# Agent attention with a maxout layer: where the transfer buffers start in SBUF

## The chip, the cores and the metric

The kernel runs on one core of a Trainium2 chip. The metric is the device time of one execution in microseconds. Three runs of the kernel before took 255.32, 255.42 and 255.44 us; the median is 255.42 us.

## The reference

Four batches of 12,544 rows with 128 features, and 49 agent rows for each batch, all in fp32:

```
a2k     = softmax(agents @ k^T / sqrt(128))      # 49 x 12544 for each batch
agent_v = a2k @ v                                # 49 x 128
q2a     = softmax(q @ agents^T / sqrt(128))      # 12544 x 49
x       = q2a @ agent_v                          # 50176 x 128 over all batches
h       = max(x @ w1, x @ w2, x @ w3)            # 50176 x 768
out     = h @ w_out                              # 50176 x 128, fp32
```

## The kernel before, in words

Every row of x is a mean over 49 rows of agent_v with weights from q2a. The kernel therefore works on the 49 rows first: for most of the 768 hidden units one of the three branches is the largest for all 49 agents, and such a unit is linear in q2a. Only the units where the winner changes, at most 64 of them for a batch, are computed for every query; all that is linear is folded into one small matrix for each batch (G). Should there be more such units, or sums out of range, a branch at the end computes everything in the general way; in the runs shown it isn't taken.

**Keys.** For each batch, k and v come in 14 groups of 6 to 8 tiles of 128 rows. A load brings two or four groups at once: 14 or 28 rows for each of 128 partitions, which lie one after the other in HBM, so one partition's share is one run of 7,168 or 14,336 bytes. GpSimd (POOL) casts k and v to bf16 (KB, VB; for the first batch ScalarE casts v), TensorE (PE) turns k, VectorE (DVE) copies it out of PSUM (KT), PE makes the scores, ScalarE (ACT) their exponentials (EK), and PE adds them up with v.

**Queries.** 48 whole groups of 8 tiles, and a 49th group that is mixed: two tiles from each batch. One load brings three groups, 24 rows or 12,288 bytes for each partition; for the mixed group four runs of 1,024 bytes. POOL casts (QB), PE turns, ACT copies (QT), PE makes scores, ACT exponentials (EQ), PE the two branches that matter, ACT and DVE their maximum (AS, R), PE the output products, and DVE multiplies by one over the row's sum and writes fp32 to OS. One store sends three groups (12,288 bytes for each partition); the last ones are smaller.

**Order.** What each engine does in which order, and which buffer of a class each piece takes, is written out in a long string (ORDER) and not found at build time. All bulk transfers are issued by SP into one queue, 71 entries: 16 loads of k and 16 of v, 4 of weights, 17 of q, 18 stores. ACT issues one small load, of the agents, at the start. An entry waits on SP until its buffer is free, and the entries behind it wait too.

**Buffers.** `SLOTS` gives the number of buffers of each class, `SHAPE` their shape. The loads share five buffers LD of 14,336 bytes for each partition, the stores five buffers OS of 12,288 bytes. Line 217 allocates all classes in the order in which they stand in `SLOTS`; the constants (lines 218 to 282) lie ahead of them in SBUF, since their pool is opened first. Lines 316 (k, v), 376 (weights), 574 (q) and 577 (out) issue the transfers.

Of the kernel before, what the change touches and what calls it, by code (L numbers as in the profile page):

```python
# [16 lines left out]
P, H, C, A, B, NT, GT, KT, NF = 128, 64, 128, 49, 4, 98, 8, 7, 6  # L17
# [14 lines left out]

PE, ACT, DVE, POOL, SP = range(5)

SLOTS = {"M": 8, "LD": 5, "QB": 3, "KB": 3, "VB": 4, "KT": 3, "QT": 3, "EQ": 8, "EK": 4, "AS": 3, "R": 3, "OS": 5}
SHAPE = {"LD": ([P, max(TK * KT, LONG), C], FP32), "QB": ([P, GT, C], BF16), "KB": ([P, GT, C], BF16), "VB": ([P, GT, VC], BF16),
         "KT": ([P, GT * C], BF16), "QT": ([P, GT, P], BF16), "EQ": ([P, 512], BF16), "EK": ([P, GT * H], BF16),
         "AS": ([P, 512], BF16), "R": ([P, 512], BF16), "OS": ([P, LONG, C], FP32)}
# [2 lines left out]
class Plan:  # L41


    def __init__(self):
        self.ops, self.index, self.tiles, self.maker = [], {}, {}, {}
# [10 lines left out]
    def places(self, order, given):  # L56

        left = {}
        for o in self.ops:
            for t in o["use"]:  # L60
                left[t] = left.get(t, 0) + 1
        free = {c: list(range(n)) for c, n in SLOTS.items()}
        place = {}
# [12 lines left out]
def parts_of(s):  # L76

    if s < B * WHOLE:
        return [(s // WHOLE, s % WHOLE * GT, GT, 0, GT // 2)]
    return [(b, WHOLE * GT, 2, b, 1) for b in range(B)]  # L80
# [129 lines left out]
class Emit:  # L210
    def __init__(self, tc, pools, io):
        nc = tc.nc
        self.tc, self.nc, self.pools, self.io = tc, nc, pools, io
        self.t, self.place = {}, {}
        const = pools["const"]
        self.psum = pools["psum"].tile([P, 8, 512], FP32, name="psum")
        self.slots = {cls: [pools["sbuf"].tile(*SHAPE[cls], name=f"{cls}{i}") for i in range(n)] for cls, n in SLOTS.items() if cls != "M"}
        self.ident = const.tile([P, P], BF16, name="ident")
        make_identity(nc, self.ident)
        self.later = const.tile([P, P], BF16, name="later")  # L220
        make_lower_triangular(nc, self.later, diag=False)
        self.ones = const.tile([P, P], BF16, name="ones")
        nc.vector.memset(self.ones, 1.0)
        self.sums_of = const.tile([P, KEYS + NQ * GT], FP32, name="sums_of")
        nc.vector.memset(self.sums_of[:, :KEYS], 1.0)
        self.ag_st, self.ag_bf = self.slots["OS"][-1][:AP_, :A // 7, :], self.slots["QT"][-1][:AP_]
        nc.vector.memset(self.ag_bf, 0.0)
        nc.scalar.dma_start(self.ag_st, io["agents"].rearrange("b a c -> (b a) c").rearrange("(p j) c -> p j c", p=AP_))
        for e in self.slots["EK"]:
            nc.vector.memset(e, 0.0)  # L230
        for v in self.slots["VB"]:
            nc.vector.memset(v[:, :, C:], 1.0)
        self.agT = const.tile([P, B, H], BF16, name="agT")
        nc.vector.memset(self.agT, 0.0)
        self.sel = const.tile([P, 2], BF16, name="sel")
        nc.vector.memset(self.sel, 0.0)
        nc.vector.memset(self.sel[:A, 0:1], 1.0)
        nc.vector.memset(self.sel[H:H + A, 1:2], 1.0)
        self.ident_of_pairs = const.tile([P, P], FP32, name="ident_of_pairs")
        nc.vector.tensor_copy(out=self.ident_of_pairs, in_=self.ident)  # L240
        self.slot_of = const.tile([P, H], FP32, name="slot_of")
        self.avT = [const.tile([P, H], BF16, name=f"avT{b}") for b in range(B)]
        self.G = [const.tile([P, GC], BF16, name=f"G{b}") for b in range(B)]
        for t in self.avT + self.G:
            nc.vector.memset(t, 0.0)  # L245
        self.wo_bf = const.tile([P, NF, C], BF16, name="wo_bf")
        self.wall = const.tile([P, WC], BF16, name="wall")
        nc.vector.memset(self.wall[:, C1O:], 0.0)
        self.cand = const.tile([P, 3, NF, A], FP32, name="cand")
        flat = self.cand.rearrange("p i f a -> p (i f a)")  # L250
        self.w1_bf = flat[:, :DFF // 2].bitcast(BF16)
        self.w1T = flat[:, DFF // 2:DFF].bitcast(BF16).rearrange("p (f c) -> p f c", c=P)
        self.av, self.even_av = flat[:A, :C // 2].bitcast(BF16), flat[:A, C // 2:C // 2 + C + 1]
        self.uv, self.rp = (const.tile([P, NF, 2, H], BF16, name=n) for n in ("uv", "rp"))
        for t in (self.uv, self.rp):
            nc.vector.memset(t, 0.0)
        self.gap3 = const.tile([P, 3 * NF], FP32, name="gap3")
        self.gap = const.tile([P, NF], FP32, name="gap")
        self.open = const.tile([P, 2 * NF - 1], FP32, name="open")
        nc.vector.memset(self.open, 0.0)  # L260
        self.upto = const.tile([P, NF], BF16, name="upto")
        self.total = self.upto[:, NF - 1:]
        self.shut = const.tile([P, NF], FP32, name="shut")
        self.counts = const.tile([P, B], FP32, name="counts")
        self.good = const.tile([P, 2], FP32, name="good")
        self.good_bf = const.tile([P, 1], BF16, name="good_bf")
        self.most = const.tile([P, 1], INT32, name="most")
# [432 lines left out]
    def queries_in_general(self):  # L700
# [13 lines left out]
        for s in range(NQ):  # L714
            parts, half = parts_of(s), slice(s % TG * GT, (s % TG + 1) * GT)
            q, out = slots["LD"][3 + s % 2], slots["OS"][s // TG % SLOTS["OS"]]
            qb, qT, e, et = (slots[cls][s % 2] for cls in ("QB", "QT", "EQ", "AS"))
# [173 lines left out]
```

## Time and profile before

| what | value |
|---|---|
| median of three runs | 255.42 us |
| the profiled execution | 255.84 us |
| its span, first to last instruction | 254.0 us |
| DMA: bytes, packets | 104.85 MB, 11,067 |
| HBM read, written | 78.74 MB, 25.69 MB |
| share of 16 DMA engines taken by SP's queue | 97.9% |
| busy: PE, DVE, ACT, POOL | 78%, 66%, 59%, 66% |

The profile page lists the span in 40 slices with the busy share of the DMA engines (in tenths) and what they moved (GB/s). A row of the windows gives the busy time of each engine in a stretch, then the clock granted to TensorE, the DMA share and GB/s; the share can be a little over 1, as one packet begins just before the other ends. In a DMA answer for a window, "packets" counts every piece that a DMA engine moves, the small ones that report completion (under 512 B) too. "DMA ... to landing" is the time from issue to the last byte, queueing included.

### The profile page before, as it was taken

The page shows a single profiled execution, that of the slowest core. Times are in us where ns is not written, and L with a number is a line of the kernel's source. Part 1 is how long each engine was busy: PE and PEld are TensorE (multiplying, and loading weights), DVE is VectorE, ACT ScalarE, POOL GpSimd, SP SyncE. Part 2 cuts the span into 40 slices and gives each one's busy share as a digit, 9 for nine tenths or more (in the row PEclk, how much of TensorE's full clock was granted, in tenths as well). Part 3 has the DMA queues.
Part 4 walks back from the last instruction along what each step waited for, and adds up shares of the span by engine and source line. Part 5 has one row for each costly group of instructions (what it writes and reads, how often), then busy time and mean ns, then how long its engine had stood idle before and what let it go on. Part 6 is the DMA issues. An engine that isn't in the chain of part 4 may idle for free.

```text
span 254.0 us, 5192 instructions
## 1 busy us (share of the span) xinstructions
PE 199.2 (78%) x1899; PEld 144.1 (57%) x1899; DVE 167.7 (66%) x379; ACT 149.9 (59%) x252; POOL 168.3 (66%) x167
## 2 busy tenths in 40 slices
PE   0674687669899889898996898988787988999910
PEld 0462455547677567676774675856564555676600
DVE  8445512667678688767688964555738889888940
ACT  2346347248666776584765866556275868777620
POOL 2363643999899399998984988579484456548000
PEclk9999567799999999999999999799999999999995
DMA  6999999999999999999999999999999999999993
GB/s 240 432 420 425 419 424 428 424 423 423 427 418 427 436 417 425 423 425 427 412 431 426 426 429 423 427 428 423 418 431 421 433 413 422 430 426 424 424 415 147
DMA packets 11067, 104.85 MB, mean 413 GB/s; under 512 B 1150, under 2 KB 2174, under 8 KB 3866
## 3 DMA queue, kind: packets, MB, share of 16 engines
q1 hardware_dynamic: 10992, 104.34, 97.9%
q8 instruction: 17, 0.28, 0.4%
q14 instruction: 16, 0.13, 0.1%
q10 hardware_dynamic: 42, 0.10, 0.1%
HBM read 78.74 MB, written 25.69 MB: 411 GB/s over the span
## 4 chain that ended last, share of the span: by engine, by line
DMA 47%; POOL 17%; PE 15%; ACT 6%; DVE 5%; issue 5%; POOLq 0%; ACTq 0%; DVEq 0%
DMA LD<-in_k_dram 38%; PE psum L294 11%; DMA LD<-in_q_dram 9%; POOL KB L329 9%; POOL VB L329 6%; PE psum L340 4%; POOL QB L586 2%; ACT QT L592 2%; ACT EQ L605 2%; DVE OS L644 1%; DVE G L245 1%; ACT AS L625 1%; DVE KT L348 1%; DVE R L628 0%; ACT OS L647 0%
## 5 line engine op out<-in xcount | busy, mean ns | idle before, releaser
L586 POOL CAST QB<-LD 128x1024 bf16<-128x1024 f32 x49 | 60.6, 1266 | 36.8 <-DMA LD<-in_q_dram 23.5
L329 POOL CAST KB<-LD 128x1024 bf16<-128x1024 f32 (+1 forms) x56 | 62.7, 1160 | 26.7 <-DMA LD<-in_k_dram 26.7
L644 DVE TENSOR_TENSOR OS<-psum,sums_of 128x512 f32<-128x512 f32 x97 | 61.0, 677 | 5.5 <-PE psum L294 3.1
L592 ACT ACTIVATE QT<-psum 128x1024 bf16<-128x1024 bf16 x49 | 50.2, 1025 | 20.2 <-PE psum L340 18.1
L348 DVE COPY KT<-psum 128x1024 bf16<-128x1024 bf16 (+1 forms) x56 | 34.4, 621 | 32.0 <-PE psum L340 25.2
L340 PE MATMUL psum<-ident_of_pairs,KB 128*128 128x128 f32 x196 | 37.0, 314 | 6.5 <-POOL KB L329 5.1
L362 ACT ACTIVATE EK<-psum 128x392 bf16<-128x392 f32 (+1 forms) x56 | 25.8, 467 | 22.7 <-PE psum L294 9.8
L625 ACT ACTIVATE AS<-psum 128x512 bf16<-128x512 f32 x49 | 29.1, 599 | 16.8 <-PE psum L294 14.3
L628 DVE TENSOR_TENSOR R<-psum,AS 128x512 bf16<-128x512 f32 x49 | 32.6, 677 | 8.1 <-ACT AS L625 4.1
L294 PE MATMUL psum<-VB,EK 128*128 128x260 bf16 x196 | 33.8, 296 | 5.3 <-ACT VB L327 3.6
L329 POOL CAST VB<-LD 128x1024 bf16<-128x1024 f32 (+1 forms) x42 | 37.6, 941 | 0.0
L605 ACT ACTIVATE EQ<-psum 128x512 bf16<-128x512 f32 x49 | 29.3, 598 | 12.8 <-PE psum L294 12.4
L294 PEld LDWEIGHTS <-EQ 128*128 128x128 bf16 x392 | 27.5, 97 | 12.8 <-ACT EQ L605 7.7
L340 PE MATMUL psum<-ident_of_pairs,QB 128*128 128x128 f32 x196 | 31.7, 285 | 3.6 <-POOL QB L586 3.4
L340 PEld LDWEIGHTS psum<-ident_of_pairs,KB 128*128 128x128 f32 x196 | 24.6, 158 | 13.6 <-POOL KB L329 12.1
L294 PE MATMUL psum<-EQ,G 128*128 128x512 bf16 (+1 forms) x104 | 31.5, 365 | 0.9 <-ACT QT L592 0.7
L294 PE MATMUL psum<-G,R 128*128 128x256 bf16 x196 | 29.4, 273 | 1.2 <-DVE R L628 1.2
L294 PE MATMUL psum<-G,EQ 128*128 128x256 bf16 x196 | 29.6, 272 | 0.2 <-DVE OS L644 0.2
L340 PEld LDWEIGHTS psum<-ident_of_pairs,QB 128*128 128x128 f32 x196 | 21.7, 142 | 11.3 <-issue 5.2
L294 PEld LDWEIGHTS <-EK 128*128 128x128 bf16 x196 | 18.3, 103 | 14.7 <-issue 6.7
L294 PE MATMUL psum<-QT,agT 128*64 128x512 bf16 (+1 forms) x104 | 19.9, 385 | 6.7 <-ACT QT L592 6.4
L294 PE MATMUL psum<-agT,KT 128*128 128x49 bf16 x392 | 20.6, 191 | 4.0 <-DVE KT L348 3.7
(96 smaller groups left out, 166.9 us busy)
## 6 DMA issues: line engine op xcount, KB each, us to landing
LD<-in_q_dram SPq DMA_DIRECT2D x16, 1536.0 KB, 18.1
out_dram<-OS SPq DMA_DIRECT2D x15, 1536.0 KB, 21.0
LD<-in_k_dram SPq DMA_DIRECT2D x12, 1792.0 KB, 16.0
LD<-in_v_dram SPq DMA_DIRECT2D x12, 1792.0 KB, 16.3
LD<-in_k_dram SPq DMA_DIRECT2D x4, 896.0 KB, 16.1
LD<-in_v_dram SPq DMA_DIRECT2D x4, 896.0 KB, 14.1
LD<-in_moe_w_dram SPq DMA_DIRECT2D x3, 384.0 KB, 13.0
out_dram<-OS SPq DMA_DIRECT2D x2, 512.0 KB, 10.8
```

Source lines behind the costliest of these rows:

```text
L245: nc.vector.memset(t, 0.0)
L294: self.nc.tensor.matmul(out, w, x, start=start, stop=True, skip_group_check=True)
L329: self.nc.gpsimd.tensor_copy(out=out, in_=src)
L340: self.nc.tensor.transpose(t[:, i * P:(i + 1) * P], two[:, i * P:(i + 1) * P], self.ident_of_pairs)
L348: self.nc.vector.tensor_copy(out=self.t[f"kT{r}"][:, :n], in_=self.t[f"kT_ps{r}"].bitcast(BF16)[:, :n])
L362: self.nc.scalar.activation(e[:, :n, :A], s, AF.Exp, scale=SCALE)
L586: return lambda: self.nc.gpsimd.tensor_copy(out=two_by_two(self.t[f"qb.{s}"], GT), in_=self.half("q", s).rearrange("p (i x) c -> p i c x", ...
L592: return lambda: self.nc.scalar.activation(self.t[f"qT.{s}"].rearrange("p (x i) n -> p x (i n)", x=2), self.t[f"qT_ps.{s}"].bitcast(BF16). ...
L605: return lambda: self.nc.scalar.activation(self.t[f"e.{s}"], self.t[f"qs.{s}"], AF.Exp, scale=SCALE)
L625: return lambda: self.nc.scalar.activation(self.t[f"a.{s}"], self.t[f"u.{s}"], AF.Relu)
L628: return lambda: self.nc.vector.tensor_tensor(out=self.t[f"r.{s}"], in0=self.t[f"v.{s}"], in1=self.t[f"a.{s}"], op=ALU.max)
L644: self.nc.vector.tensor_tensor(out=out, in0=src, in1=rc.unsqueeze(2).to_broadcast([P, 4, C]), op=ALU.mult)
```

## The change

`SLOTS` names OS right behind LD, so the five store buffers follow the five load buffers in SBUF; all classes that stood between move up by 61,440 bytes. A constant tile of 192 bytes, which nothing reads or writes, moves everything that is allocated behind it by 192 bytes. Start addresses, in bytes of a partition, from the allocation of the two built programs:

| buffer | before | past a multiple of 256 / 512 | after | past a multiple of 256 / 512 |
|---|---|---|---|---|
| LD0 | 39,232 | 64 / 320 | 39,424 | 0 / 0 |
| LD4 | 96,576 | 64 / 320 | 96,768 | 0 / 0 |
| OS0 | 162,240 | 192 / 448 | 111,104 | 0 / 0 |
| OS4 | 211,392 | 192 / 448 | 160,256 | 0 / 0 |
| QB0 | 110,912 | 64 / 320 | 172,544 | 0 / 0 |
| R2 | 161,216 | 192 / 448 | 222,848 | 128 / 128 |
| agT | 18,880 | 192 / 448 | 19,072 | 128 / 128 |

LD1 to LD3 and OS1 to OS3 lie between at whole multiples of 512 from their neighbours. On every engine the instructions, their order and their waits are the same in both programs; only addresses differ, and lines behind the inserted one have a number that is higher by one.

```
-SLOTS = {"M": 8, "LD": 5, "QB": 3, "KB": 3, "VB": 4, "KT": 3, "QT": 3, "EQ": 8, "EK": 4, "AS": 3, "R": 3, "OS": 5}
+SLOTS = {"M": 8, "LD": 5, "OS": 5, "QB": 3, "KB": 3, "VB": 4, "KT": 3, "QT": 3, "EQ": 8, "EK": 4, "AS": 3, "R": 3}
...
         self.sums_of = const.tile([P, KEYS + NQ * GT], FP32, name="sums_of")
+        const.tile([P, 192], mybir.dt.uint8, name="pad")
         nc.vector.memset(self.sums_of[:, :KEYS], 1.0)
```

## The prediction

> **What bounds the kernel now.** I read the page first, for the DMA engines, because the change moves buffers that only transfers of q, k, v, the weights and the output fill and empty in bulk.
>
> ```profile
> DMA  6999999999999999999999999999999999999993
> GB/s 240 432 420 425 419 424 428 424 423 423 427 418 427 436 417 425 423 425 427 412 431 426 426 429 423 427 428 423 418 431 421 433 413 422 430 426 424 424 415 147
> DMA packets 11067, 104.85 MB, mean 413 GB/s; under 512 B 1150, under 2 KB 2174, under 8 KB 3866
> q1 hardware_dynamic: 10992, 104.34, 97.9%
> ```
>
> In 38 of 40 slices the 16 DMA engines are busy nine tenths or more, and one queue's packets (q1, SP's) alone take 97.9% of what 16 engines have over the span. Next come the windows (columns: PE, PEld, DVE, ACT, POOL busy with counts, granted clock, DMA share, GB/s), to see whether any stretch has another limit.
>
> ```profile
> core 0: us, PE busy (x) PEld busy (x) DVE busy (x) ACT busy (x) POOL busy (x), PEclk, DMA share, GB/s
> 30.00:40.00 10.00, 7.55 (x61) 5.25 (x59) 2.37 (x4) 5.20 (x9) 5.17 (x5) 0.67 1.01 426
> 50.00:60.00 10.00, 7.12 (x81) 5.29 (x80) 6.68 (x20) 6.17 (x14) 9.98 (x10) 1.00 0.99 419
> 180.00:200.00 20.00, 15.43 (x143) 10.86 (x141) 13.54 (x28) 10.98 (x18) 11.26 (x10) 1.00 1.01 428
> 220.00:230.00 10.00, 9.59 (x91) 6.55 (x90) 8.86 (x18) 8.21 (x13) 4.75 (x4) 1.00 1.01 424
> 240.00:245.00 5.00, 2.45 (x19) 1.48 (x16) 4.38 (x14) 1.74 (x5) 0.00 (x0) 1.00 1.03 417
> 245.00:250.00 5.00, 0.00 (x0) 0.00 (x0) 0.00 (x0) 0.00 (x0) 0.00 (x0) 0.74 0.87 357
> ```
>
> Where POOL is full (50 to 60 us) or PE nearly so (220 to 230 us), the DMA share is still about 1: the queue is never empty behind them. After 245 us no engine computes and the transfers still run. So the time is what the DMA engines need for 104 MB, and compute only has to issue early enough. The chain and SP's queue say the same of the end:
>
> ```profile
> 132.48 22.03 DMA LD<-in_k_dram
> 159.00 23.04 DMA LD<-in_q_dram
> ...
> 243.51 1.14 ACT OS L647 x4
> ```
>
> ```profile
> L574 SPq DMA_DIRECT2D LD<-in_q_dram x17: 327/328/3565, 35.0 to 198.1; - x17
> L577 SPq DMA_DIRECT2D out_dram<-OS x18: 332/398/3442, 68.8 to 244.7; - x18
> DMA packets 384, 2.47 MB, mean 247 GB/s; under 512 B 46, under 2 KB 56, under 8 KB 184
> out_dram<-OS SPq DMA_DIRECT2D x1, 512.0 KB, 8.4
> ```
>
> The first two rows say when SP issued its loads of q and its stores, first and last (us). The other two are of the window 244 to 254 us: 2.47 MB were still to move when the last store was issued at 244.7 us, 5.8 us at 424 GB/s, and that store landed 8.4 us after its issue. The chain leaves the DMA at 182 us (159.00 + 23.04) for a compute stretch, but this backlog lies behind it. A DMA that is up to about 4 us faster over the program ends about that much earlier; one that is slower ends later in full. Nothing else covers it.
>
> **The change part by part.** No instruction, wait, queue entry or byte is added or removed; only start addresses move. Compute tiles move by 192 bytes (the constants behind the pad) or by 61,632 (QB to R), and OS moves by -51,136. All three are multiples of 64 (3, 963 and 799 times), so no engine operand changes its place within 64 bytes. I price this part at nothing; if it cost, the rows above say that compute may finish some 4 us later before the backlog is gone. SP still issues the same 71 entries in the same order, and the pad is written by nobody.
>
> What can move is the cost of a run, the contiguous piece (one per partition, or several) that a DMA engine moves as one packet. The issues give the number of runs:
>
> ```profile
> LD<-in_q_dram SPq DMA_DIRECT2D x16, 1536.0 KB, 18.1
> out_dram<-OS SPq DMA_DIRECT2D x15, 1536.0 KB, 21.0
> LD<-in_k_dram SPq DMA_DIRECT2D x12, 1792.0 KB, 16.0
> LD<-in_v_dram SPq DMA_DIRECT2D x12, 1792.0 KB, 16.3
> LD<-in_k_dram SPq DMA_DIRECT2D x4, 896.0 KB, 16.1
> LD<-in_v_dram SPq DMA_DIRECT2D x4, 896.0 KB, 14.1
> LD<-in_moe_w_dram SPq DMA_DIRECT2D x3, 384.0 KB, 13.0
> out_dram<-OS SPq DMA_DIRECT2D x2, 512.0 KB, 10.8
> out_dram<-OS SPq DMA_DIRECT2D x1, 1024.0 KB, 9.3
> LD<-in_q_dram SPq DMA_DIRECT2D x1, 512.0 KB, 22.1
> LD<-in_moe_w_out_dram SPq DMA_DIRECT2D x1, 384.0 KB, 13.5
> ```
>
> Loads: 16 + 24 + 8 + 4 = 52 with 128 runs, and the 512 KB one of q with 4 x 128, so 7,168 or 448 for each engine. Stores: 15 + 1 + 1 with 128, and one of the two 512 KB stores (the mixed group) with 512, so 2,688 or 168 for each engine. Together 616.
>
> What a run costs beyond its bytes comes from three windows: loads alone (30 to 65 us), the mixed group's load, which has runs of 1,024 bytes (206 to 208 us), and stores alone (225 to 235 us; the last load of q, issued at 198.1 us, has landed by then, 26.8 us later by its row).
>
> ```profile
> DMA packets 1207, 14.89 MB, mean 426 GB/s; under 512 B 129, under 2 KB 129, under 8 KB 131
> q1 hardware_dynamic: 1202, 14.84, 100.3%
> DMA packets 309, 0.80 MB, mean 398 GB/s; under 512 B 16, under 2 KB 265, under 8 KB 265
> q1 hardware_dynamic: 309, 0.80, 100.8%
> DMA packets 390, 4.28 MB, mean 428 GB/s; under 512 B 42, under 2 KB 42, under 8 KB 42
> q1 hardware_dynamic: 389, 4.26, 100.6%
> DMA to landing us min/median/max: 26.8/26.8/26.8
> ```
>
> Stores: 10 us x 16 x 1.006 = 161.0 engine-us for 389 - 42 = 347 runs of 12,288 bytes, 463.9 ns each with its share of the small completion packets. The middle window: 2 x 16 x 1.008 = 32.26 engine-us for 265 - 16 = 249 runs of 1,024 bytes and 44 of 12,288; 32.26 - 44 x 0.4639 leaves 47.6 ns for a short run. The slope is (463.9 - 47.6) / 11,264 = 0.0370 ns a byte, and a run of no bytes would cost 47.6 - 37.9 = 9.7 ns. That is all that a start address can be charged with here: at most 616 x 9.7 ns = 6.0 us. The other end is nothing, or below it (the second rival).
>
> Which end is nearer? Before the change every load run starts 64 bytes past a multiple of 256, every store run 192 past. Loads alone: 35 x 16 x 1.003 = 561.7 engine-us for 1,073 runs of 13,830 bytes on average, 523.5 ns, of which the slope explains 511.2 and 12.3 ns are left (1,207 - 129 less the 5 packets of other queues are the 1,073 runs). Two quite different misplacements therefore have remainders that are close, 12.3 and 9.7 ns, and the order is the wrong one: a cost by misplaced bytes would make the stores 128 x 0.0370 = 4.7 ns dearer, and they are 2.6 ns cheaper. A cost common to both, or one of the loads alone, cannot be excluded from these rows, as no run here starts on a boundary. I take nothing, because the one comparison of two placements that the trace offers speaks against a charge, and keep 6.0 us for the range. A gain of 0.51 us (0.2%, the least this kernel's measurement tells from no change) needs 0.83 ns a run.
>
> By the Trainium skill, "DMA: Bandwidth & Descriptors", section "How a descriptor splits into AXI transactions", a read begins at the multiple of 256 bytes below its start, and the bytes ahead of the start are fetched for nothing and still take their beats. Taken for both directions, it is the second form of the first rival. The same page (section "Where 436 GB/s comes from") puts the ports' ceiling at 435 GB/s; beside the 426 measured, this leaves some 2%, an estimate of 5 us from that figure; the trace agrees in size with its bound of 6.0 us.
>
> Sum: 0 for compute, 0 for issue, 0 for the runs. The profiled execution took 255.84 us, its span 254.0, so 1.84 us lie around it; the median of the runs is 255.42, 0.42 below the profiled one, and the forecast stands at the median: **255.4 us**, with 255.0 to 255.8 as its own range.
>
> **The rivals.** First, a run that starts off a boundary is charged for the misplaced bytes, and the change takes that away. If only loads pay (their target is SBUF, and their remainder is the higher one), the price is the 64 misplaced bytes, 64 x 0.0370 = 2.4 ns: 448 runs make 1.1 us, so 254.3 us. For it speaks that loads are dearer by just 2.6 ns; against it, that loads also have another source, HBM, which can explain the same, and that the difference of two remainders from rounded shares is no sharp number. If both pay, stores at 192 x 0.0370 = 7.1 ns, 168 runs add 1.2 us: 255.4 - 1.1 - 1.2 = 253.1 us. Against this stands the stores' remainder of 9.7 ns, of which 2.6 would be left for the rest, where loads keep 9.9.
>
> Second, on the other side: after the change all ten buffers start at the same place within 512 bytes, where loads stood at 320 and stores at 448. If a write to one and a read of another meet more often in the same part of a partition's memory, transfers of both directions slow each other. The place is the mixed stretch, from the first store (68.8 us) to the last load's issue (198 us), 129 us. The price I take from the slowest loads-only row above, 419 GB/s, against some 425: 1.4% of 129 us, 1.8 us, so 257.2 us. It decides from 0.4% on (0.51 of 129 us), as no other work covers the queue. Against it: five load buffers share one phase today, and reads of POOL and writes of DMA at that phase show no loss at 426 GB/s.
>
> Third, that the change doesn't do what it says, would leave 255.4 as well; the built program's addresses are multiples of 512, so I give it no chance of its own.
>
> **How the numbers follow.** No effect that can be measured 0.46; loads alone gain 0.24 (254.3); loads and stores gain, or more up to the bound, 0.13 (253.1 and below); slower 0.17, by the second rival or something like it in a part of its size. So faster by over 0.2% (below 254.9) has 0.37, within 0.2% 0.46, slower 0.17. The range goes from 252.9, which holds the first rival in both forms, to 256.6, which holds the second rival up to two thirds of its price: **252.9 to 256.6 us**.
>
> **What would show it.** In the profile after, the rows of the same three kinds of windows: loads alone, short runs, stores alone. I expect remainders again near 12 and 10 ns, 426 GB/s, and 97.9% for q1. If the loads' remainder falls by some 2.4 ns and the stores' does not, the first form of the first rival holds; if both fall, the second. If only mixed windows lose GB/s, it is the second rival. The largest groups of compute should keep their means (677, 1160 and 1266 ns) to a per cent:
>
> ```profile
> L644 DVE TENSOR_TENSOR OS<-psum,sums_of 128x512 f32<-128x512 f32 x97 | 61.0, 677 | 5.5 <-PE psum L294 3.1
> L329 POOL CAST KB<-LD 128x1024 bf16<-128x1024 f32 (+1 forms) x56 | 62.7, 1160 | 26.7 <-DMA LD<-in_k_dram 26.7
> L586 POOL CAST QB<-LD 128x1024 bf16<-128x1024 f32 x49 | 60.6, 1266 | 36.8 <-DMA LD<-in_q_dram 23.5
> ```
>
> Wrong altogether would be a time that moves while all these remainders stay: then compute or issue limits a stretch in which I read the queue as full.

## The result, and the profile after

The changed kernel takes 254.29 us (median of 14 runs) against 255.6 for the kernel before in the same comparison; the ratio of the one to the other is 0.9934, 95% interval 0.9915 to 0.9953. So it is faster by 0.66%, 1.7 us (1.2 to 2.2). The ratio is of the means of the undisturbed runs (254.14 and 255.82 us); two slow runs of the changed kernel, of 259.67 and 263.2 us, count in its median alone, so the medians lie only 1.3 us apart. The time lies in the range and 1.1 us below the forecast of 255.4; the first form of the first rival, "loads alone gain", had 254.3.

The page of the changed kernel, its DMA lines:

```profile
DMA  6999999999999999999999999999999999999994
DMA packets 11067, 104.85 MB, mean 416 GB/s; under 512 B 1150, under 2 KB 2174, under 8 KB 3866
q1 hardware_dynamic: 10992, 104.34, 98.1%
```

The same packets and bytes, the engines as full as before, and a higher rate: each packet has become cheaper. The windows say where. First three stretches of the kernel before, then of the changed one (last two columns: DMA share, GB/s):

```profile
10.00:65.00 55.00, 40.55 (x382) 29.96 (x381) 26.42 (x53) 29.46 (x53) 36.32 (x34) 0.84 1.01 424
65.00:180.00 115.00, 102.22 (x1036) 76.09 (x1034) 82.32 (x177) 73.93 (x127) 96.24 (x93) 0.99 1.01 424
180.00:240.00 60.00, 51.90 (x459) 34.65 (x458) 47.73 (x105) 42.43 (x66) 32.22 (x31) 1.00 1.01 425
```

```profile
10.00:65.00 55.00, 40.20 (x386) 29.07 (x386) 26.06 (x54) 30.35 (x53) 36.93 (x35) 0.91 1.01 428
65.00:180.00 115.00, 101.14 (x1021) 75.06 (x1030) 82.74 (x178) 73.25 (x126) 95.41 (x92) 0.99 1.01 428
180.00:240.00 60.00, 52.44 (x452) 35.35 (x457) 46.67 (x103) 42.41 (x66) 32.27 (x31) 0.97 1.01 426
```

424 has become 428 GB/s as long as loads make up most of the queue, and 425 only 426 in the last stretch, where the loads run out and stores fill it. The DMA answers for windows give it by run. Of the changed kernel, loads alone (30 to 65 us), then stores alone (226 to 236 us):

```profile
DMA packets 1213, 15.02 MB, mean 429 GB/s; under 512 B 128, under 2 KB 128, under 8 KB 128
q1 hardware_dynamic: 1208, 14.96, 100.3%
DMA packets 384, 4.23 MB, mean 423 GB/s; under 512 B 40, under 2 KB 40, under 8 KB 40
q1 hardware_dynamic: 383, 4.21, 99.5%
```

Loads: 35 x 16 x 1.003 = 561.7 engine-us for 1,208 - 128 = 1,080 runs of 13,852 bytes, 520.1 ns a run, where 523.5 ns stood for 13,830 bytes. The 22 bytes more are worth 0.8 ns at the prediction's 0.0370 ns a byte, so a load run is 4.2 ns cheaper. Stores: 159.2 engine-us for 343 runs, 464.1 ns where 463.9 stood: unchanged. From 10 to 65 us, with more runs, the same for the kernel before and the changed one:

```profile
DMA packets 2322, 23.32 MB, mean 424 GB/s; under 512 B 256, under 2 KB 256, under 8 KB 768
q1 hardware_dynamic: 2316, 23.24, 100.5%
...
DMA packets 2336, 23.52 MB, mean 428 GB/s; under 512 B 256, under 2 KB 256, under 8 KB 768
q1 hardware_dynamic: 2330, 23.44, 100.4%
```

256 packets of each are completion reports. 884.4 engine-us for 2,060 runs are 429.3 ns, of which 12.3 remain when the bytes (11,282 at 0.03696 ns, 417.0 ns) are taken off; 883.5 for 2,074 runs are 426.0, and 8.3 remain. So 4.0 ns less for each load run; 448 runs for each DMA engine make 1.8 us, which is the measured gain within its interval. The remainders themselves hang on the slope, which joins short load runs to long store runs; what counts here is their difference between two kernels.

Compute didn't change and didn't gain. The largest groups of the changed kernel keep their means (1264, 1154 and 678 ns for 1266, 1160 and 677), and its last piece of work starts at 243.59 us, where the kernel before had it at 243.51 (below, in this order: the groups, the end of the chain, the landing of the stores):

```profile
L587 POOL CAST QB<-LD 128x1024 bf16<-128x1024 f32 x49 | 60.6, 1264 | 37.1 <-DMA LD<-in_q_dram 21.1
L330 POOL CAST KB<-LD 128x1024 bf16<-128x1024 f32 (+1 forms) x56 | 62.5, 1154 | 26.5 <-DMA LD<-in_k_dram 26.0
L645 DVE TENSOR_TENSOR OS<-psum,sums_of 128x512 f32<-128x512 f32 x97 | 61.0, 678 | 5.0 <-PE psum L295 3.1
...
243.59 1.14 ACT OS L648 x4
...
DMA to landing us min/median/max: 5.7/17.9/26.2
```

The last row is of the stores: the quickest to land, which is the last one, now needs 5.7 us instead of 8.4. So the gain came out of the backlog behind the last compute.

### The profile page after: what moved, and what is told of

The parts are those of the page before. It is cut to its first block, busy times and chain, and to the rows that moved or that the text cites. A ratio compares the mean times of both kernels' runs of the same rounds, so it can differ in the third digit from the quotient of the medians.

```text
span 252.0 us, 5173 instructions
## 1 busy us (share of the span) xinstructions
PE 198.4 (79%) x1880; PEld 142.9 (57%) x1899; DVE 166.8 (66%) x379; ACT 150.1 (60%) x252; POOL 167.9 (67%) x167
## 4 chain that ended last, share of the span: by engine, by line
DMA 48%; POOL 17%; PE 12%; ACT 5%; issue 4%; DVE 2%; POOLq 0%; ACTq 0%; DVEq 0%
DMA LD<-in_k_dram 31%; DMA LD<-in_q_dram 17%; PE psum L295 10%; POOL KB L330 9%; POOL VB L330 7%; PE psum L341 2%; ACT QT L593 2%; POOL QB L587 1%; ACT EQ L606 1%; DVE OS L645 1%; ACT cand L391 1%; DVE R L629 0%; ACT OS L648 0%; ACT AS L626 0%; DVE G L550 0%
## 5 line engine op out<-in xcount | busy, mean ns | idle before, releaser
L587 POOL CAST QB<-LD 128x1024 bf16<-128x1024 f32 x49 | 60.6, 1264 | 37.1 <-DMA LD<-in_q_dram 21.1
L330 POOL CAST KB<-LD 128x1024 bf16<-128x1024 f32 (+1 forms) x56 | 62.5, 1154 | 26.5 <-DMA LD<-in_k_dram 26.0
L593 ACT ACTIVATE QT<-psum 128x1024 bf16<-128x1024 bf16 x49 | 50.2, 1024 | 20.0 <-PE psum L341 19.2
L341 PE MATMUL psum<-ident_of_pairs,KB 128*128 128x128 f32 x196 | 35.6, 306 | 5.0 <-POOL KB L330 3.2
L363 ACT ACTIVATE EK<-psum 128x392 bf16<-128x392 f32 (+1 forms) x56 | 25.8, 467 | 20.9 <-PE psum L295 12.5
L295 PE MATMUL psum<-VB,EK 128*128 128x260 bf16 x196 | 33.1, 291 | 6.1 <-ACT VB L328 4.1
L295 PEld LDWEIGHTS <-EQ 128*128 128x128 bf16 x392 | 28.2, 98 | 13.0 <-ACT EQ L606 7.6
L295 PE MATMUL psum<-G,R 128*128 128x256 bf16 x196 | 30.7, 281 | 1.2 <-DVE R L629 1.2
L295 PE MATMUL psum<-G,EQ 128*128 128x256 bf16 x196 | 31.1, 282 | 0.0
L341 PEld LDWEIGHTS psum<-ident_of_pairs,KB 128*128 128x128 f32 x196 | 23.6, 153 | 12.3 <-POOL KB L330 9.8
L295 PE MATMUL psum<-EQ,G 128*128 128x512 bf16 (+1 forms) x85 | 25.8, 363 | 1.9 <-ACT QT L593 0.7
```

The source lines that it names most:

```text
L295: self.nc.tensor.matmul(out, w, x, start=start, stop=True, skip_group_check=True)
L330: self.nc.gpsimd.tensor_copy(out=out, in_=src)
L341: self.nc.tensor.transpose(t[:, i * P:(i + 1) * P], two[:, i * P:(i + 1) * P], self.ident_of_pairs)
L363: self.nc.scalar.activation(e[:, :n, :A], s, AF.Exp, scale=SCALE)
L587: return lambda: self.nc.gpsimd.tensor_copy(out=two_by_two(self.t[f"qb.{s}"], GT), in_=self.half("q", s).rearrange("p (i x) c -> p i c x", ...
L593: return lambda: self.nc.scalar.activation(self.t[f"qT.{s}"].rearrange("p (x i) n -> p x (i n)", x=2), self.t[f"qT_ps.{s}"].bitcast(BF16). ...
```

## The experiments

The three theories of the first four: **A**, only where a load's run starts in SBUF counts; **B**, loads and stores both pay for a start off a boundary; **C**, the store buffers' place next to the load buffers does it. In each case the remainder of a run is worked out from q1's row of 10 to 65 us as above (packets less 256; share x 880 engine-us; less 0.03696 ns a byte, the slope of the prediction unrounded). A rounded share is good to about 0.2 ns and the rounded MB to 0.1 ns.

**The pad alone** (`SLOTS` as in the kernel before; loads at multiples of 512, stores 128 past a multiple of 256):

```
+        const.tile([P, 192], mybir.dt.uint8, name="pad")
```

> The pad alone: load buffers at multiples of 512, store buffers stay last, now 128 past a multiple of 256. Theory A (only where a load's run starts in SBUF counts, some 4 ns for each of 448 load runs an engine): all of the gain, ratio to before about 0.993, q's queue moves 23.44 MB in 10 to 65 us as in the changed kernel (23.24 before). Theory B (loads and stores both pay for a start off a boundary): only part of it, the stores 128 past still pay; 0.995 or above. Theory C (the store buffers' place next to the load buffers brings it, not the boundary): ratio 1.000, 23.24 MB.

Measured: 253.89 us, ratio 0.9922 (0.9893 to 0.9951), the whole gain. Its row of 10 to 65 us:

```profile
q1 hardware_dynamic: 2334, 23.50, 100.5%
```

884.4 / 2,078 runs is 425.6 ns, remainder 7.6. That is A's figure; the move of the store buffers isn't needed.

**Stores alone on the boundary**, by 64 bytes ahead of them at their old place:

```
-SLOTS = {..., "R": 3, "OS": 5}
+SLOTS = {..., "R": 3, "PAD": 1, "OS": 5}
-         "AS": ([P, 512], BF16), "R": ([P, 512], BF16), "OS": ([P, LONG, C], FP32)}
+         "AS": ([P, 512], BF16), "R": ([P, 512], BF16), "PAD": ([P, 16], FP32), "OS": ([P, LONG, C], FP32)}
```

> Store buffers alone at multiples of 512, by 64 bytes of padding ahead of them at their old place; load buffers as before, 64 past a multiple of 256. Theory A: ratio 1.000, 23.24 MB in 10 to 65 us, a store run 464 ns in 225 to 235 us. Theory B: faster by up to 0.5% (168 store runs an engine at 7 ns are 1.2 us), a store run some 457 ns. Theory C: 1.000.

Measured: 255.36 us, ratio 0.9984 (0.9965 to 1.0003), no difference that this comparison tells. Rows of 10 to 65 us and of 226 to 236 us:

```profile
q1 hardware_dynamic: 2316, 23.24, 100.5%
...
DMA packets 393, 4.26 MB, mean 426 GB/s; under 512 B 47, under 2 KB 47, under 8 KB 47
q1 hardware_dynamic: 392, 4.24, 100.1%
```

The load row is to the digit that of the kernel before, and a store run costs 160.2 / 345 = 464.2 ns, as it did 192 bytes past a boundary (463.9). B falls: stores, which read SBUF, pay nothing.

**The order alone** (OS behind LD, no pad; all ten 64 past a multiple of 256):

```
-SLOTS = {"M": 8, "LD": 5, "QB": 3, ..., "R": 3, "OS": 5}
+SLOTS = {"M": 8, "LD": 5, "OS": 5, "QB": 3, ..., "R": 3}
```

> Store buffers behind the load buffers without the pad: all ten 64 past a multiple of 256, 320 past one of 512. Theory A: ratio 1.000, 23.24 MB in 10 to 65 us. Theory B: 1.000 or a little faster, as stores go from 192 to 64 past. Theory C: all of the gain, 0.993. The rival that equal phases of loads and stores slow the mixed stretch: slower than before, at a DMA rate below 424 GB/s in 65 to 180 us.

Measured: 255.89 us, ratio 0.9988 (0.9968 to 1.0008). Rows of 10 to 65 us and 65 to 180 us:

```profile
q1 hardware_dynamic: 2315, 23.23, 100.5%
...
DMA packets 4404, 48.79 MB, mean 424 GB/s; under 512 B 490, under 2 KB 490, under 8 KB 1037
```

Remainder 12.5 ns, as before: C falls. Here all ten buffers stand at one phase, with loads and stores mixed from 68.9 us on, and the rate is the 424 GB/s that the kernel before has there: the prediction's second rival falls as well, at this phase; in the changed kernel, with all ten on the boundary, that stretch rose to 428.

**Multiples of 256 alone** (the changed kernel with 448 bytes of padding, all ten 256 past a multiple of 512):

```
-        const.tile([P, 192], mybir.dt.uint8, name="pad")
+        const.tile([P, 448], mybir.dt.uint8, name="pad")
```

> As the changed kernel, with 448 bytes of padding in place of 192: all ten buffers at 256 past a multiple of 512, that is at multiples of 256 alone. If the boundary that counts is 256 or less: ratio 0.993, 23.44 MB in 10 to 65 us. If it is 512: ratio 1.000 or above, 23.24 MB or less.

Measured: 253.87 us, ratio 0.9919 (0.9893 to 0.9945).

```profile
q1 hardware_dynamic: 2334, 23.50, 100.5%
```

Remainder 7.6 ns. 512 isn't the boundary; 256 is enough.

**How the charge goes with the distance.** Three kernels differ from the changed one in the pad alone: 320 bytes (128 past a multiple of 256), 128 bytes (192 past) and 224 bytes (32 past); the first is shown.

```
-        const.tile([P, 192], mybir.dt.uint8, name="pad")
+        const.tile([P, 320], mybir.dt.uint8, name="pad")
```

> As the changed kernel with 320 bytes of padding: all ten buffers 128 past a multiple of 256. Theory A1 (a load run pays for the bytes between the boundary of 256 below it and its start): twice the charge of 64 bytes, 8 ns a run, 3.6 us over the changed kernel, ratio to before 1.007, 23.04 MB in 10 to 65 us. Theory A2 (a fixed charge for any start off a multiple of 256): as before, 1.000, 23.24 MB. Theory A3 (the boundary that counts is 128): as the changed kernel, 0.993, 23.5 MB.

> As the changed kernel with 128 bytes of padding: all ten buffers 192 past a multiple of 256. Theory A1: three times the charge, 12 ns a run, 5.4 us over the changed kernel, ratio to before 1.014, 22.85 MB in 10 to 65 us. Theory A2: as before, 1.000, 23.24 MB. Theory A3: 64 past a multiple of 128, as before, 1.000, 23.24 MB. The stores stand where they stood before, 192 past.

> As the changed kernel with 224 bytes of padding: all ten buffers 32 past a multiple of 512. Compute tiles behind the pad move by 32 within 64 bytes as well. Theory A1: half the charge, 2 ns a run, 0.9 us over the changed kernel, ratio to before 0.997, 23.35 MB in 10 to 65 us. Theory A2 and A3: the full fixed charge, 1.000, 23.24 MB; more than that if the boundary of 64 counts too, 1.003 or above.

Measured: 255.43 us, ratio 0.9987 (0.9963 to 1.0011) at 128 past; 256.41 us, 0.9997 (0.9977 to 1.0017) at 192 past; 256.63 us, 1.0026 (1.0002 to 1.0051) at 32 past. Rows of 10 to 65 us in the same order:

```profile
q1 hardware_dynamic: 2317, 23.26, 100.5%
...
q1 hardware_dynamic: 2314, 23.21, 100.4%
...
q1 hardware_dynamic: 2315, 23.23, 100.7%
```

| load runs start past a multiple of 256 by | kernel | ns a run | remainder, ns | one run of 14,336 bytes, ns | ratio to before |
|---|---|---|---|---|---|
| 0 | changed | 426.0 | 8.3 | 535.0 | 0.9934 |
| 0 | the pad alone | 425.6 | 7.6 | 535.0 | 0.9922 |
| 0 (256 past 512) | pad 448 | 425.6 | 7.6 | 535.0 | 0.9919 |
| 32 | pad 224 | 430.4 | 13.4 | 540.8 | 1.0026 |
| 64 | before | 429.3 | 12.3 | 539.7 | 1 |
| 64 | stores alone | 429.3 | 12.3 | 539.8 | 0.9984 |
| 64 | order alone | 429.5 | 12.5 | 539.7 | 0.9988 |
| 128 | pad 320 | 429.1 | 12.0 | 538.9 | 0.9987 |
| 192 | pad 128 | 429.3 | 12.5 | 539.7 | 0.9997 |

The last column but one is the mean of the longest load runs, from the trace's records of single packets (runs that took over 1.2 times the median are left out, 0.5% of these at most, and some 4% at most of the other lengths below). Two levels, and about a nanosecond within the upper one: A2. A charge by misplaced bytes (A1) would put 192 three times as high as 64, and the 128 boundary (A3) would bring the gain at 128. At 32 past, a run costs about 1 ns more than at 64 and the ratio lies just over 1, and at 128 past the longest runs are 0.8 ns cheaper; with one trace of each, and compute tiles 32 past a multiple of 64 in the first, what this last nanosecond is stays open.

An engine that reads the load buffers isn't needed for the charge: POOL's first cast starts at 6.0 us (6.2 in the changed kernel), and of the runs of 7,168 bytes that began before 5.9 us the median is 278 ns in the kernel before and 272 in the changed one.

**A charge for each run, or for the bytes?** A fixed 4 ns for runs of some 14 KB could also be 0.9% of the bytes. So each load of k, v and whole q was issued as two, with half of each partition's run, once off the boundary (from the kernel before) and once on it (from the changed kernel; the halves are multiples of 256 long). The edit for k and v, which q has in the same way but for its mixed group:

```
-            self.nc.sync.dma_start(self.t[f"{which}{b}.{g}"][:, :n * KT, :], src)
+            cut = n * KT // 2
+            self.nc.sync.dma_start(self.t[f"{which}{b}.{g}"][:, :cut, :], src[:, :cut, :])
+            self.nc.sync.dma_start(self.t[f"{which}{b}.{g}"][:, cut:n * KT, :], src[:, cut:, :])
```

> The kernel before with each load of k, v and whole q issued as two, each with half of every partition's run: 832 load runs an engine in place of 448, all still 64 past a multiple of 256. Theory P (the charge is 4.0 ns for each load run that starts off a multiple of 256, above some 5 ns for any run): 384 runs more at 9 ns make 3.4 us more than the kernel before, ratio 1.013, and 3.3 us more than its aligned twin. Theory Q (the charge goes with the bytes written, 0.9% of them whatever the runs): 384 runs at 5 ns make 1.9 us more than before, ratio 1.007, and 1.8 us more than the aligned twin.

> The changed kernel with the same halved loads, whose runs all start at multiples of 256: 832 load runs an engine. Both theories: some 2 us over the changed kernel (384 runs at 5 ns), ratio to the kernel before about 1.001. Theory P: 3.3 us below the twin off the boundary, and the DMA of 10 to 65 us moves 1.5% more than it does there. Theory Q: 1.8 us below it, and 0.9% more.

Measured: 259.66 us off the boundary, ratio 1.0153 (1.0119 to 1.0187); 256.33 us on it, 1.0011 (0.9987 to 1.0035). The difference is 3.3 us by the medians and 3.6 by the ratios (2.6 or more, with both intervals taken together), where whole runs differ by 1.7: P, which had 3.3, and not Q, which had 1.8. The profiled execution of the kernel on the boundary took 261.56 us and moved only 387 GB/s from 10 to 65 us, so the rows compared are of 65 to 180 us, and the times decide. First off, then on:

```profile
DMA packets 8033, 48.03 MB, mean 418 GB/s; under 512 B 889, under 2 KB 889, under 8 KB 7512
q1 hardware_dynamic: 8021, 47.87, 101.0%
...
DMA packets 8209, 48.75 MB, mean 424 GB/s; under 512 B 913, under 2 KB 913, under 8 KB 7743
q1 hardware_dynamic: 8195, 48.57, 101.1%
```

1.5% more bytes on the boundary, with whole runs it was 0.9% of the loads. By run: 1,858.4 / 7,132 = 260.6 ns against 1,860.2 / 7,282 = 255.5 ns, remainders 12.5 and 9.0 ns. The 3.5 ns between them are a mean over loads and the few stores of that stretch, so about 4 ns for a load, with runs of half the length. Halving also shows what a run costs on the boundary: the kernel on it is 2.0 us slower than the changed one (256.33 - 254.29; by the ratios 2.0 as well, 0.8 either way), for 384 runs and 48 completion reports more for each DMA engine, about 5 ns a run (3 to 7).

The charge isn't the same for every length, though. Load runs taken one by one, in the kernel before and the changed one:

| bytes of the run | before, ns | changed, ns | difference, ns |
|---|---|---|---|
| 1,024 | 47.4 | 46.0 | 1.4 |
| 3,072 | 124.1 | 121.0 | 3.1 |
| 7,168 | 276.3 | 272.4 | 3.9 |
| 12,288 (before the first store) | 464.0 | 460.0 | 4.0 |
| 14,336 | 539.7 | 535.0 | 4.7 |

It grows with the run, but far less than the run does, so it is neither the same for each nor a share of the bytes. With the number of runs of each length, the mean is 4.0 ns and the sum 1.8 us for each DMA engine, the figures found above. Nor is it one value within a length: on the boundary 3,054 of the 3,072 longest runs took 535 ns to the nanosecond, off it eight tenths of them lie between 536 and 545.

## Why the prediction was right, and where it was wrong

The time lies in the range only because the range was drawn wide enough to hold the rivals. The forecast itself, no effect, with 255.0 to 255.8 as its own range and a chance of 0.46, missed; what happened is a rival that had 0.24.

**What bounds the kernel**: right. The queue was full, every nanosecond of a run went to the end, and compute was neither touched nor in the way. That a gain of up to about 4 us would pass by the backlog held for the 1.7 us: last compute at the same time, the last store landing in 5.7 us for 8.4.

**Compute and issue at nothing**: right; groups and their means are the same, and shifts by 61,440 bytes alone (the order alone) or of everything by other multiples of 64 made no difference.

**The runs at nothing**: wrong, and this is the step that failed: "I take nothing, because the one comparison of two placements that the trace offers speaks against a charge". The comparison set loads 64 past a boundary beside stores 192 past it and took them for two placements of one thing. They are not: stores read SBUF and pay nothing at any of 0, 64, 128 and 192 past (463 to 464 ns each time), loads write it and pay (4.0 ns on average). What the trace did show was the 2.6 ns by which loads were dearer, and the prediction gave that to HBM as well as to the target. It was the charge. It looked smaller than it is because loads and stores are not equal without it: on the boundary a load run keeps 520.1 - 13,852 x 0.03696 = 8.1 ns, 1.6 less than the stores' 9.7, so 4.2 ns of charge left only 2.6 to be seen. Single runs of 12,288 bytes say the same: loads 464.0 ns before and 460.0 after, stores 461.5 and 461.7 (those that began from 226 us on). Why a load without the charge is the cheaper one no run shows.

**The first rival, loads alone**: right in its place and in who pays, with 254.3 us for 254.29. Its price was mis-sized in kind: 2.4 ns for 64 misplaced bytes. Measured are 4.0 ns on average, the same within a nanosecond at 64, 128 and 192, so it is not a price by misplaced bytes. That its time met the median is luck: it took 1.1 us off 255.42, and the gain is 1.7 us, from a kernel before that stood higher in the comparison.

**By the Trainium skill**, "DMA: Bandwidth & Descriptors", section "How a descriptor splits into AXI transactions", a read starts at a multiple of 256 bytes. The same unit is right here for the writes of the loads: 512 and 128 are not the boundary. What it says of the cost, beats for the bytes ahead of the start of a read, isn't seen: reads of SBUF at 64, 128 and 192 past cost the 463 to 464 ns of those on the boundary, and the charge on writes is the same for 64 and 192. Worked out from its rule, a run of a multiple of 256 bytes, as all of these are, has one transaction more off the boundary, wherever in the 256 bytes it starts. A charge for that one transaction has the form of the rows by distance, not of the differences by length (1.4 to 4.7 ns), and no run here shows transactions.

**The first rival's second form (both pay), and the second rival**: both fell, the one with the stores alone, the other with the order alone.

## What to carry to other kernels

Where the DMA queue is full, let what loads write in SBUF start at a multiple of 256 bytes in each partition: 192 bytes of padding at the right place were worth 1.7 us here, and the buffers of stores need nothing of the kind. The charge comes with each run and grows far less than the run (3.1 ns on 121 at 3,072 bytes, 4.7 on 535 at 14,336), so it weighs more the shorter the runs are: 3.3 us where the same bytes came in runs of half the length. When a trace has two groups with different misplacements, ask first if they move in the same direction before one is taken as the other's control.

## What the runs showed of the hardware that was not expected

- A load's run that starts off a multiple of 256 bytes in SBUF cost 4 ns more on average, whether 64, 128 or 192 past (at 64 past, 1.4 ns for 1,024 bytes and 4.7 for 14,336). 256 past a multiple of 512 cost nothing (0.9919).
- A store's run cost 463 to 464 ns for 12,288 bytes at 0, 64, 128 and 192 past: these starts in SBUF don't matter when it is read. At 64, 128 and 192 past (226 to 236 us; the order alone, pad 320, pad 128):

```profile
q1 hardware_dynamic: 388, 4.23, 99.8%
...
q1 hardware_dynamic: 390, 4.24, 100.1%
...
q1 hardware_dynamic: 393, 4.25, 100.4%
```

  With 44, 45 and 47 completion reports taken off, 159.7 / 344, 160.2 / 345 and 160.6 / 346 are 464.2, 464.2 and 464.3 ns. The same window gives 462.9 for the pad alone (128 past) and 462.6 for pad 448 (0 past), so it tells kernels apart to about 1.5 ns; single store runs of 12,288 bytes from 226 us on average 461.5 to 462.0 ns in these kernels and the one before, whatever the start.
- Runs of 1,024 bytes pay less. In the mixed group's load of the changed kernel (205 to 207 us), 32.1 engine-us less 40 long runs at 0.4641 us leave 45.8 ns for each of 296 short ones, 1.8 ns below the 47.6 of the kernel before. The ends of a window of 2 us weigh about a nanosecond there; taken one by one, these runs differ by 1.4 ns (46.0 and 47.4):

```profile
DMA packets 349, 0.79 MB, mean 397 GB/s; under 512 B 13, under 2 KB 309, under 8 KB 309
q1 hardware_dynamic: 349, 0.79, 100.4%
```

- Each run on the boundary still costs about 5 ns beyond its bytes (2.0 us for 384 runs more, 3 to 7 ns). The remainders of 8 to 9 ns in the rows are higher; these rows count the overlap of neighbouring packets too (shares of up to 101.1%), and which of the two is nearer stays open.
